# Retention and SoLU feed-forward on one Trainium2 core: the carried state without its zeros, scores and state product in 64x64 quarter arrays, and a new written-out order

## The chip, the cores and the metric

One kernel on one core of a Trainium2 chip. Everything runs in one launch: the inputs lie in the chip's memory, the output goes back there, and the time is device microseconds from the start to the end of one execution. Before the change: median 212.06 us of 3 runs (211.68 to 212.1). The core has a matrix engine (PE, with its weight loads shown as PEld), a vector engine (DVE), an activation engine (ACT), a general engine (POOL) and SP, which here only issues transfers. Each engine works its own list of instructions in order.

## What is computed

Two stages, the second on the output of the first. The attention part is retention: scores weighted by a fixed decay per head, no softmax. There are 8 batches, 8 heads, 576 positions, 64 numbers per head; the feed-forward part has 4608 tokens of 512 and a hidden width of 1024.

```python
scores = q @ k.T / 8                               # per batch and head
Dmat   = where(i >= j, gamma[h] ** (i - j), 0)     # gamma[h] = 1 - 2**(-5-h)
x      = (scores * Dmat) @ v                       # heads side by side: 4608 x 512
h      = x @ w_in                                  # 4608 x 1024
solu   = h * softmax(h)
ln     = (solu - mean) / sqrt(var + 1e-6) * g_ln
out    = ln @ w_out                                # 4608 x 512
```

## The kernel before, in words

**Chunks.** The 4608 tokens are cut into 36 chunks of 128. Two batches form a group of nine chunks: for each of the four stretches of 128 positions one chunk of each batch, and a ninth chunk that holds the last 64 positions of both batches, interleaved. Numbers 8, 17, 26 and 35 are such ninth chunks. Within a batch the retention is done in stretches: inside a chunk by scores, across chunks by a carried state of 64 x 64 per head.

**What one chunk goes through.** Names are those of the steps in the code, and of the tokens in the order. `ld` issues three loads (q, k, v as float32, 256 KB each) on SP. `cq`, `ck`, `cv` make float16 of them, with the decay factors multiplied in for q and v. `tq` transposes q and k on PE in pairs of heads (16 matmuls with an identity); `tr` does only q, for chunks whose k is transposed by a DMA issued in `kd`. `eq` and `er` copy the transposes to `qkT`. `sc` (line 366) computes the scores of 8 heads, `mk` masks them on DVE. `kv` (line 389) multiplies k and v into `kp`, the state's increment; `ad` adds it to the carried state, giving `t`; `dk` (line 417) makes of `t` the float16 state `s16` for the next chunk and `d3` (line 430) the float32 one. `av` (line 441) adds masked scores times v into the accumulator `x`, and `fs` (line 455) adds state times q into the same accumulator. `ex` copies `x` out as `xT`; `m1` multiplies with w_in (for the first chunks in rows, `mr`); `mx`, `xp`, `so`, `sq`, `ra`, `rp` are the maximum, the exponential, the product and the normalisation; `tu` and `eu` transpose the result (`du` does it by DMA for the last chunks); `m2` multiplies with w_out, `st` scales and stores. The last chunk runs the feed-forward in halves (`hm` to `hw`). `wu` are matmuls on a tile of zeros that only keep PE busy at the start, `gt` and `c2` turn the vector g_ln, `li`, `wi`, `lo`, `wo`, `mm`, `mc`, `ws` bring in the weights, convert them and take the mean out of w_out.

**How PE's array is used.** Nearly all products are written as two half products, `HALF` (line 248): the stationary operand has 128 rows and 64 columns, and the two halves give output partitions 0 to 63 and 64 to 127 (`product`, line 255, `turn`, line 250). The profile writes such a group `128*64`. `sc` is the exception: the depth of one head is 64, so it takes 64 rows and 128 columns (`64*128` in the profile), even heads from partitions 0 to 63 into one PSUM bank and odd heads from 64 to 127 into another. `fs` is of the `128*64` kind because its state is kept with zeros: for a pair of heads, `s16` is 128 x 128 with the two 64 x 64 states on the diagonal and zeros beside them. `dk` writes those zeros anew for each chunk, by multiplying with a table `gd` that has them.

**What sets the order.** Nothing is scheduled by the compiler. `ORDER` is a written-out list of tokens `step:chunk[:engine]`, and each engine gets its instructions in the order in which the tokens name them. The letter picks the engine for steps that can run on more than one (a: ACT, v: DVE, g: POOL). SP's list of loads, stores and DMA transposes follows from it as well. `BANKS` gives the PSUM bank for each product in turn, `SLOTS` the buffer for each tile of a ring; `BY_PE` names the chunks from 12 on whose k is transposed by PE instead of by DMA.

Of the kernel before, what the change touches and what calls it, by code (L numbers as in the profile page):

```python
# [29 lines left out]
eq:4:a sc:4 so:1 d3:2 ad:4 ld:3 ck:3:a cq:3:g tq:3 dk:2 ce:1 xp:0 m1:2 mk:4 cv:3:g kv:3 ld:5  # L30
cq:5:g av:4 fs:4 ck:5:g eq:3:a sq:1 so:0 ad:3 ld:6 sc:3 lo:0 cv:5:g ck:6:g ex:4:a tq:5 eq:5:a
cq:6:g mx:2 xp:2 mk:3 dk:3 ce:0 cv:6:g lo:2 m1:4 tu:1 mx:4 sc:5 wu:1:2 eu:1:a mk:5 d3:4 d3:3 av:3
fs:3 xp:4 so:2 tu:0 av:5 wo:1:g ex:3:a kv:5 fs:5 ce:2 tq:6 lo:1 so:4 eu:0:a wo:4:g ce:4 eq:6:a
m1:3 sc:6 ad:5 ex:5:a kv:6 ad:6 wo:3:a wo:2:a lo:3 m1:5 wo:6:v ld:7 tu:2 wo:7:g wo:0:a ld:8 wo:5:a
sq:2 ra:1:g tu:4 mk:6 rp:1 ld:12 mx:3 ld:9 eu:2:v m2:1 sq:0 dk:6 ld:10 dk:4 sq:4 cq:8:g eu:4:v
m2:0 cq:7:v st:1 ck:7:a xp:3 ra:0:v cv:7:v mx:5 so:3 mm:0 ld:11 rp:0 st:0 tq:7 mc:0:v av:6 ld:13
eq:7:a fs:6 ex:6:a m2:2 sc:7 ra:2:g ck:8:g ws:0:v dk:5 ce:3 rp:2 tq:8 xp:5 d3:5 mk:7 so:5 cv:8:g
eq:8:a ra:4:v ws:4:v ws:7:v st:2 m1:6 tu:3 sc:8 mk:8 m2:4 ck:9:g rp:4 sq:3 kv:7 eu:3:a m2:3 cq:9:g
ws:6:v ad:7 dk:7 mx:6 ws:2:g sq:5 ws:5:v ra:3:v rp:3 ws:1:v st:4 ra:5:g cq:11:v av:7 fs:7 ex:7:a
ck:10:g ld:17 tu:5 eu:5:a xp:6 rp:5 ws:3:v cv:9:g av:8 cq:10:g cq:12:g fs:8 ex:8:v so:6 ck:12:g  # L40
tr:9 m1:7 m2:5 ck:11:g er:9:av st:3 tu:6 sc:9 mx:7 m1:8 st:5 eu:6:v xp:7 kd:12 kv:9 ld:14 mk:9
so:7 av:9 sq:6 ex:9:a tr:10 er:10:a cv:10:g ad:9 d3:9 ra:6:v rp:6 cq:13:g sq:7 ra:7:g ck:13:g
kd:13 m2:6 st:6 mx:8 cv:13:g tu:7 eu:7:a sc:10 mk:10 m1:9 kv:10 ad:10 dk:10 tr:11 xp:8 so:8 av:10
ex:10:a tr:12 er:12:v cv:12:g er:11:a m2:7 tu:8 dk:9 sc:11 mx:9 m1:10 cv:11:g mk:11 av:11 fs:11
ld:15 sq:8 rp:7 ra:8:v eu:8:a kv:11 d3:10 xp:9 cq:17:g rp:8 ex:11:a st:7 m2:8 so:9 tu:9 ad:11
d3:11 dk:11 mx:10 sc:12 cq:14:g ck:14:a kd:14 sq:9 m1:11 eu:9:v xp:10 ck:15:g ld:16 st:8 kv:12
mk:12 ld:19 ra:9:v cv:17:g tr:14 er:14:a tr:13 ad:12 dk:12 so:10 av:12 fs:12 ex:12:a cv:14:g
er:13:a m2:9 sc:13 mx:11 rp:9 xp:11 mk:13 cq:16:g tu:10 eu:10:a ck:17:v m1:12 so:11 sc:14 st:9
mk:14 av:13 ck:16:g sq:10 fs:13 ex:13:a m2:10 ra:10:g rp:10 mx:12 d3:12 kv:13 ad:13 cq:15:g tu:11
dk:13 eu:11:v sq:11 kv:14 kd:16 d3:13 ld:18 ra:11:v rp:11 st:10 m1:13 xp:12 ck:19:g tr:15 er:15:a  # L50
ld:21 av:14 ad:14 cv:19:g fs:14 ex:14:a tr:16 er:16:a m2:11 so:12 cv:15:g sc:15 mx:13 mk:15 tu:12
xp:13 m1:14 dk:14 st:11 so:13 eu:12:a cv:16:g kv:15 d3:14 ad:15 sc:16 mk:16 av:15 fs:15 ck:18:g
sq:13 kd:18 mx:14 m2:12 kv:16 ex:15:a tr:17 sq:12 ad:16 ra:12:g rp:12 ra:13:v av:16 fs:16 ld:20
xp:14 ex:16:a tu:13 er:17:v m1:15 so:14 ck:21:g sc:17 eu:13:a mx:15 kd:19 tu:14 st:12 dk:16 mk:17
eu:14:a xp:15 so:15 ld:22 m2:13 cq:18:g tr:18 er:18:a av:17 dk:15 fs:17 ck:20:v ex:17:a m1:16
cq:19:v ld:23 rp:13 st:13 tu:15 sc:18 mx:16 sq:14 ra:14:v eu:15:a m2:14 mk:18 cv:18:g xp:16 so:16
rp:14 cq:21:g cq:20:g st:14 tr:19 er:19:a kd:21 sq:15 ra:15:g rp:15 cq:22:g kv:18 ad:18 m1:17
mx:17 av:18 sq:16 sc:19 mk:19 m2:15 ex:18:a cv:20:g d3:18 ld:24 xp:17 kv:19 ad:19 d3:19 dk:18
tu:16 tr:20 er:20:v tr:21 so:17 cv:21:g eu:16:a er:21:a m1:18 ck:22:g kd:22 av:19 st:15 cq:23:g
# [24 lines left out]
st:26 mx:32 er:35:av ex:34:a sc:35 ad:34 mx:33 xp:32 sq:29 ra:29:g so:32 xp:33 ra:28:g rp:28 du:32
m2:28 rp:29 ra:30:v so:33 du:33 m2:29 dk:34 mk:35 m1:34 mx:34 st:28 sq:31 m2:30 av:35 dk:33 fs:35
sq:32 ex:35:v xp:34 so:34 ra:31:g m2:31 du:34 sq:33 ra:32:v rp:30 hm:35:0 hx:35:0 st:30 hm:35:1
st:29 hx:35:1 m2:32 rp:31 st:31 sq:34 hp:35:0 ho:35:0 ra:33:g hp:35:1 rp:33 ho:35:1 hc:35 m2:33
rp:32 st:32 ht:35:0 he:35:0:v ht:35:1 ra:34:g he:35:1:v hq:35:0:v rp:34 hq:35:1:a ra:35:g st:33
m2:34 st:34 rp:35 h2:35:0 hw:35:0:a h2:35:1 hw:35:1:v
# [13 lines left out]
qf 012345601234560135426015324601532460  # L103
kf 012345012345012453014523014520314520
vf 012345601234560134625016342051346250
q16 012340123401324103123041203412304132
v16 012341023410234132012041320421320413
k16 012345120345102341502314053210452310
qkT 012301230123013120321302310231032103
# [748 lines left out]
```

## Time and profile before

| | |
|---|---|
| median of 3 runs | 212.06 us (211.68 to 212.1) |
| the profiled execution | 212.6 us, of which 210.9 us from the first to the last instruction |
| mean granted clock of PE | 0.997 |
| PE busy | 195.6 us, 93% of the span |
| weight loads (PEld) busy | 124.6 us, 59% |
| DVE busy | 177.8 us, 84% |
| ACT busy | 167.4 us, 79% |
| POOL busy | 166.5 us, 79% |
| moved by DMA | 46.94 MB, mean 223 GB/s |

How to read the rows of the trace: a group of a view by lines shows line, engine, operation, output and inputs, shapes and count, then busy time and the mean of one, then idle time before it and what ended that. A row of the timeline shows the start, the time from the first start to the last end in the row, the engine, the instruction and its count. Matmuls overlap in the pipeline, so the time that a group of matmuls really takes is read from its start to the start of the group behind it, not from its length. In a table by stage, each engine has its busy time and, in brackets, its count of instructions.

### The profile page before, as it was taken

How to read it: one execution, taken by the hardware profiler on the slowest of the kernel's cores; microseconds unless marked ns; L12 is line 12 of the kernel's file. 1: busy time of each engine (PE TensorE's matmuls, PEld its weight loads, DVE VectorE, ACT ScalarE, POOL GpSimd, SP SyncE). 2: the span in 40 equal slices, each digit the busy share in tenths (PEclk: the TensorE clock that was granted, in tenths of full speed). 3: DMA queues.
4: the chain of work that ended last, by engine and by line, in shares of the span. 5: the costliest groups of instructions: out<-in, count | busy, mean ns of one | idle time of the engine just before them, and what ended most of it. 6: DMA issues, size and time to landing. Idle time of an engine off the chain costs nothing.

```text
span 210.9 us, 7674 instructions
## 1 busy us (share of the span) xinstructions
PE 195.6 (93%) x3173; PEld 124.6 (59%) x3173; DVE 177.8 (84%) x312; ACT 167.4 (79%) x289; POOL 166.5 (79%) x244
## 2 busy tenths in 40 slices
PE   0985699999999999999999999999999999999992
PEld 0463467656756666666666656676666666565552
DVE  0474899999998799979898899999989998999650
ACT  2333689989759997988899788888798897798982
POOL 5284898998798998996928999799999975938531
PEclk9999999999999999999999999999999999999998
DMA  5999899999998899999999799999999995999264
GB/s 134 263 324 276 208 243 333 276 219 249 238 236 234 215 218 253 250 222 287 190 227 252 178 221 226 188 251 195 210 271 223 170 210 153 174 168 280 69 215 152
DMA packets 110931, 46.94 MB, mean 223 GB/s; under 512 B 95656, under 2 KB 104880, under 8 KB 110896
## 3 DMA queue, kind: packets, MB, share of 16 engines
q1 hardware_dynamic: 110576, 46.28, 96.7%
q8 instruction: 25, 0.41, 0.9%
q10 hardware_dynamic: 320, 0.16, 0.3%
q14 instruction: 10, 0.08, 0.1%
HBM read 32.54 MB, written 9.44 MB: 199 GB/s over the span
## 4 chain that ended last, share of the span: by engine, by line
PE 75%; SPq 12%; DMA 6%; POOL 2%; issue 1%; ACT 1%; DVE 0%; POOLq 0%; DVEq 0%
PE o L258 28%; PE h L258 24%; SPq L272 6%; PE lp L253 5%; SPq L276 5%; PE sc L373 4%; DMA qf<-in_q_dram 4%; PE x L448 3%; PE x L258 3%; DMA kf<-in_k_dram 2%; PE tr L253 2%; PE tp L253 2%; SPq L771 1%; PE kp L397 1%; PE oh L258 1%
## 5 line engine op out<-in xcount | busy, mean ns | idle before, releaser
L258 PE MATMUL h<-w_in,xT 128*64 128x512 f16 x560 | 66.7, 380 | 1.4 <-DVE w_in L245 1.4
L258 PE MATMUL o<-w_c,uT 128*64 128x512 f16 x480 | 56.8, 380 | 0.0
L386 DVE TENSOR_TENSOR ret<-sc,tris 128x512 f16<-128x512 f32 x72 | 46.1, 681 | 3.3 <-PE sc L373 2.5
L258 PEld LDWEIGHTS <-xT 128*64 128x64 f16 x576 | 31.6, 110 | 24.4 <-issue 1.9
L510 ACT ACTIVATE e<-h,nm 128x1024 f32<-128x1024 f32 x35 | 39.3, 1123 | 7.5 <-DVE nm L504 6.5
L519 DVE SCALAR_TENSOR_TENSOR u<-h,e 128x1024 f16<-128x1024 f32 x35 | 42.6, 1217 | 2.7 <-ACT e L510 2.2
L504 DVE TENSOR_REDUCE nm<-h 128x1 f32<-128x1024 f32 x35 | 42.6, 1217 | 2.1 <-PE h L258 1.8
L258 PEld LDWEIGHTS <-uT 128*64 128x64 f16 x560 | 30.4, 110 | 23.6 <-issue 0.2
L292 POOL TENSOR_TENSOR q<-qf,small 128x512 f16<-128x512 f32 x31 | 32.4, 1051 | 6.8 <-DMA qf<-in_q_dram 6.8
L424 POOL TENSOR_TENSOR s<-t,small 128x512 f16<-128x512 f32 x32 | 33.9, 1063 | 3.5 <-DVE t L412 3.3
L547 ACT ACTIVATE sq<-u,su 128x1024 bf16<-128x1024 f16 x30 | 34.6, 1154 | 1.2 <-DVE u L519 1.1
L281 POOL TENSOR_TENSOR v<-vf,small 128x512 f16<-128x512 f32 x32 | 33.9, 1063 | 1.8 <-DMA vf<-in_v_dram 1.8
L607 ACT ACTIVATE o_sb<-o,rs 128x512 f32<-128x512 f32 x35 | 24.1, 694 | 7.3 <-POOL rs L573 3.8
L573 POOL TENSOR_TENSOR rs<-w,mhalf 128x1 f32<-128x1 f32 x36 | 20.9, 581 | 5.8 <-DVE w L564 3.7
L245 ACT CAST xT<-x 128x512 f16<-128x512 f32 x32 | 18.6, 588 | 5.1 <-PE x L258 4.2
L245 ACT COPY uT<-lp 128x1024 f16<-128x1024 f16 x17 | 17.3, 1019 | 0.7 <-PE lp L253 0.7
L245 POOL CAST k<-kf 128x512 f16<-128x512 f32 x24 | 14.6, 611 | 4.0 <-DMA kf<-in_k_dram 3.9
L253 PE MATMUL lp<-ident,u 128*64 128x128 f16 x448 | 17.1, 220 | 0.1
L436 POOL TENSOR_TENSOR s<-t,small 128x256 f32<-128x256 f32 x24 | 15.0, 630 | 2.1 <-DVE t L412 1.5
L448 PE MATMUL x<-ret,v 128*64 128x128 f16 x288 | 15.2, 225 | 1.3 <-DVE ret L386 1.2
L253 PEld LDWEIGHTS <-q 128*64 128x64 f16 x280 | 10.7, 115 | 9.0 <-POOL q L292 6.5
L245 ACT COPY qkT<-tp 128x512 f16<-128x512 f16 x24 | 13.2, 598 | 3.4 <-PE tp L253 3.3
(88 smaller groups left out, 267.0 us busy)
## 6 DMA issues: line engine op xcount, KB each, us to landing
qf<-in_q_dram SPq DMA_DIRECT2D x36, 256.0 KB, 4.2
kf<-in_k_dram SPq DMA_DIRECT2D x36, 256.0 KB, 4.6
vf<-in_v_dram SPq DMA_DIRECT2D x36, 256.0 KB, 5.0
out_dram<-o_sb SPq DMA_DIRECT2D x35, 256.0 KB, 4.1
w_in<-in_moe_w_in_dram SPq DMA_DIRECT2D x4, 512.0 KB, 7.4
w_out<-in_moe_w_out_dram SPq DMA_DIRECT2D x4, 512.0 KB, 6.2
qkT<-k SPq DMA_TRANSPOSE x19, 4.3
out_dram<-o_sbh ACTq DMA_DIRECT2D x2, 64.0 KB, 2.2
```

The source lines that it names most:

```text
L245: (engine.copy if engine is nc.scalar else engine.tensor_copy)(out=out, in_=in_)
L253: nc.tensor.transpose(out=out[w], in_=in_[:, w], identity=ident)
L258: nc.tensor.matmul(out=out[w], lhsT=lhsT[:, w], rhs=rhs, start=start, stop=stop, skip_group_check=True,)
L281: engine.tensor_tensor(out=dst, in0=T.pop((key, n)), in1=table.unsqueeze(2).to_broadcast([P, H, D]), op=ALU.mult,)
L292: ENG[e].tensor_tensor(out=dst.rearrange("p (a h) d -> p h a d", h=2), in0=T.pop(("qf", n)).rearrange("p (h a) d -> p h a d", h=2), in1=ta ...
L386: nc.vector.tensor_tensor(out=r, in0=s, in1=m, op=ALU.mult)
L424: nc.gpsimd.tensor_tensor(out=s16, in0=t.unsqueeze(2).to_broadcast([P, 4, 2, D]), in1=gd.unsqueeze(3).to_broadcast([P, 4, 2, D]), op=ALU.mult,
L504: nc.vector.tensor_reduce(out=nm, in_=T["h", n], axis=AX.X, op=ALU.max, negate=True)
L510: nc.scalar.activation(out=e, in_=T["h", n], func=ACT.Exp, bias=T.pop(("nm", n)), accum_out=s)
L519: nc.vector.scalar_tensor_tensor(out=u, in0=T.pop(("h", n)), scalar=-1.0, in1=T.pop(("e", n)), op0=ALU.mult, op1=ALU.mult, accum_out=su,)
L547: nc.scalar.activation(out=s, in_=T.pop(("v", n)), func=ACT.Square, scale=-float(DFF), bias=T.pop(("su", n)), accum_out=ss,)
L607: nc.scalar.activation(out=o_sb, in_=T.pop(("o", n)), func=ACT.Copy, scale=T.pop(("rs", n)))
```

## The change

Four things change together.

1. `dk` no longer writes zeros: `s16` becomes 128 x 4 x 64 (the two heads' states one under the other), and the table `gd` goes.
2. `fs` takes the state in quarters: for each pair of heads, rows 0 to 63 give output partitions 0 to 63 and rows 64 to 127 give 64 to 127. The number of matmuls stays 8 (16 in a ninth chunk).
3. `sc` is cut once more along its columns: 16 matmuls of 64 x 64 in place of 8 of 64 x 128.
4. `BY_PE` names four chunks (13, 16, 20, 24) in place of two (15, 20), and `ORDER`, `BANKS` and `SLOTS` are written anew as a whole, with other engines for many steps.

```diff
-BY_PE = (15, 20)
+BY_PE = (13, 16, 20, 24)
...
-        gd[e * 64 : e * 64 + 64, :, e] = gs[e * 64 : e * 64 + 64]
-    small = np.concatenate([gq, gk, gqt, gkt, gs, gd.reshape(P, 8), gqm, par], axis=1).astype(np.float32)
+    small = np.concatenate([gq, gk, gqt, gkt, gs, gqm, par], axis=1).astype(np.float32)
...
     def sc(n):
...
-                nc.tensor.matmul(
-                    out=s[e][:, hp], lhsT=qkT[dd, 1, hp], rhs=qkT[dd, 0, hp],
-                    start=True, stop=True,
-                )
+                for w in HALF:
+                    nc.tensor.matmul(
+                        out=s[e][w, hp], lhsT=qkT[dd, 1, hp, w], rhs=qkT[dd, 0, hp],
+                        start=True, stop=True,
+                    )
...
     def dk(n):
...
-        s16 = ring(stp, [P, 4, 2, D], F16, "s16")
+        s16 = ring(stp, [P, 4, D], F16, "s16")
         nc.gpsimd.tensor_tensor(
-            out=s16, in0=t.unsqueeze(2).to_broadcast([P, 4, 2, D]),
-            in1=gd.unsqueeze(3).to_broadcast([P, 4, 2, D]), op=ALU.mult,
+            out=s16, in0=t, in1=gs.unsqueeze(2).to_broadcast([P, 4, D]), op=ALU.mult
         )
...
     def fs(n):
...
-                product(
-                    part(T["x", n][:, hp], i), s[:, hp].rearrange("p e d -> p (e d)"),
-                    part(qkT[:, 0, hp], i), False, i == len(s16) - 1,
-                )
+                for w in HALF:
+                    nc.tensor.matmul(
+                        out=part(T["x", n][w, hp], i), lhsT=s[w, hp],
+                        rhs=part(qkT[w, 0, hp], i), start=False, stop=i == len(s16) - 1,
+                        skip_group_check=True,
+                    )
```

Two stretches of the order, before and after, from the middle (chunks 12 to 17):

```
before:  ... tr:16 er:16:a m2:11 so:12 cv:15:g sc:15 mx:13 mk:15 tu:12 xp:13 m1:14 dk:14 ... av:15 fs:15 ck:18:g ...
after:   ... av:15 fs:15 rp:12 sc:16 mx:14 ... m2:13 ex:16:v tu:14 ... av:17 fs:17 ex:17:a sq:15 mx:16 sc:18 m2:14 ...
```

Counted over the whole list, PE has 36 `sc` and 28 `fs` in both. In the new list 14 of the `fs` stand directly beside an `sc` among PE's steps, four stand beside another `fs` (two pairs), and ten stand alone. The first nine loads (chunks 1, 0, 2, 4, 3, 5, 6, 7, 8) and the weights among them keep their places on SP, except that the four parts of w_in come in the order 3, 0, 2, 1 (before 2, 3, 0, 1) and the last two of w_out are swapped; behind that the loads come in another order. DMA transposes of keys go from 19 to 17. Of the steps that can move, ACT converts 16 keys (before 9), POOL 15 (before 24), DVE 5 (before 3).

More of the change, by code (lines that the diff above doesn't have):

```diff
@@ L30 @@
[L30 to L59, printed above, removed]
@@ L84 @@
[L84 to L89, printed above, removed]
+c1:0 wu:5:2 ld:1 ld:0 wu:3:2 gt:0 c2:0 cq:1:g ck:1:a tq:1 wu:4:2 eq:1:a ld:2 cv:1:v cq:0:v ck:0:a
@@ new lines @@
+kv:1 sc:1 mk:1 tq:0 eq:0:v li:3 cv:0:g ad:1 cv:2:g kv:0 ad:0 dk:0 d3:0 sc:0 ck:2:a wu:2:2 cq:2:v
+mk:0 li:0 wi:3:0:v tq:2 li:2 eq:2:a av:0 av:1 ex:1:v li:1 kv:2 ad:2 ld:4 d3:1 d3:2 ex:0:a wi:3:1:a
+wi:0:0:a wi:0:1:v sc:2 mk:2 ld:3 mr:1:3 dk:2 mr:0:0 wi:1:0:v ld:5 wi:2:1:a mr:1:0 av:2 dk:1 fs:2
+ex:2:v wi:2:0:a ck:4:a ld:6 mr:1:2 wi:1:1:g mr:1:1 cq:4:g lo:0 mr:0:2 mr:0:1 mr:0:3 tq:4 mx:1 xp:1
+mx:0 eq:4:a cv:4:g so:1 kv:4 cq:3:g ck:3:g sc:4 ad:4 cv:3:g cq:5:g tq:3 ce:1 ck:5:g m1:2 cv:5:g
+kv:3 lo:2 xp:0 mk:4 so:0 ad:3 av:4 fs:4 ce:0 d3:3 lo:3 lo:1 eq:3:a sc:3 mx:2 d3:4 tq:5 sq:1 ck:6:g
@@ new lines @@
+ex:4:a m1:4 eq:5:a dk:3 tu:1 mk:3 av:3 mx:4 sc:5 dk:4 mk:5 xp:2 eu:1:a fs:3 ex:3:a wu:1:2 so:2
+xp:4 so:4 tu:0 kv:5 ad:5 cq:6:g cv:6:g ce:4 av:5 fs:5 ex:5:a ld:7 tq:6 eq:6:a m1:3 ce:2 kv:6 sc:6
+ld:8 wo:6:v eu:0:a ad:6 wo:1:g m1:5 wo:0:a mk:6 wo:4:g ld:10 tu:2 ld:9 tu:4 eu:4:v ra:1:g ld:12
+wo:5:a wo:3:a wo:7:g wo:2:a cq:7:g sq:4 m2:1 mx:3 ck:7:a eu:2:v sq:0 rp:1 tq:7 eq:7:a cv:7:g xp:3
+mx:5 ra:0:v rp:0 dk:5 m2:0 st:0 av:6 cq:8:g sq:2 fs:6 ex:6:v mm:0 so:3 m2:2 ce:3 ld:11 mc:0:v sc:7
+ws:4:v cv:8:v st:1 ck:8:a tq:8 mk:7 xp:5 so:5 ws:0:v m1:6 ra:2:g dk:6 rp:2 ra:4:g eq:8:a sc:8 st:2
@@ new lines @@
+cq:9:g mk:8 tu:3 eu:3:a d3:5 rp:4 m2:4 st:4 ws:7:v kv:7 ad:7 tu:5 eu:5:a ck:9:g ld:13 ws:6:v
+ws:1:v tr:9 er:9:av av:7 fs:7 m2:3 cv:10:g cq:12:g mx:6 dk:7 av:8 fs:8 ws:5:v ws:2:g ex:7:a sc:9
+m1:7 sq:3 ra:3:g ex:8:a xp:6 sq:5 ws:3:v m2:5 mk:9 so:6 tu:6 ld:14 rp:3 cv:9:g st:3 ra:5:v ck:12:v
+mx:7 sq:6 eu:6:v av:9 ex:9:a cq:10:g xp:7 kv:9 ad:9 rp:5 cq:11:g st:5 ra:6:g dk:9 kd:12 ck:10:v
+m1:8 tr:10 er:10:a m2:6 so:7 sq:7 rp:6 mx:8 sc:10 tu:7 eu:7:a st:6 cv:12:v m1:9 xp:8 mk:10 kv:10
+ad:10 ck:11:g cq:14:g tr:11 ra:7:g tr:12 cv:11:g av:10 ex:10:a rp:7 dk:10 ld:15 m2:7 so:8 d3:9
@@ new lines @@
+tu:8 er:11:av mx:9 er:12:a sc:11 m1:10 st:7 kv:11 mk:11 eu:8:a xp:9 ad:11 sq:8 av:11 fs:11 sc:12
+cq:13:g ex:11:a m2:8 so:9 sq:9 mx:10 kv:12 d3:10 cv:14:g cv:13:g ad:12 ld:16 ck:14:g kd:14 m1:11
+ra:8:g tr:14 ck:13:a rp:8 st:8 ck:15:a mk:12 tu:9 av:12 fs:12 tr:13 kd:15 ld:17 xp:10 ra:9:v
+cq:15:v ex:12:a eu:9:v m2:9 er:13:a so:10 er:14:a sc:13 ld:19 rp:9 st:9 tu:10 d3:11 cv:16:g m1:12
+mx:11 mk:13 xp:11 cq:16:g d3:12 av:13 dk:12 so:11 eu:10:a ld:22 sc:14 cv:15:v dk:11 fs:13 sq:10
+ra:10:g ld:18 ck:16:a ex:13:a rp:10 mk:14 sq:11 ra:11:g mx:12 xp:12 m2:10 kv:13 ad:13 dk:13 kv:14
@@ new lines @@
+ad:14 d3:13 tu:11 m1:13 eu:11:v so:12 st:10 av:14 fs:14 ex:14:a tr:16 er:16:a ld:21 tr:15 m2:11
+er:15:v mx:13 xp:13 sc:15 dk:14 ck:17:g cq:19:g ck:19:g rp:11 cq:17:g st:11 cv:17:g tu:12 eu:12:a
+m1:14 ck:22:g mk:15 so:13 kv:15 ad:15 sq:12 ra:12:g d3:14 av:15 fs:15 rp:12 sc:16 mx:14 cq:22:g
+ex:15:a xp:14 cv:18:g ck:18:a kd:18 m2:12 kv:16 cq:18:g ld:20 mk:16 tu:13 dk:15 tr:17 m1:15 kd:19
+ad:16 eu:13:v er:17:a st:12 dk:16 so:14 sq:13 ra:13:g mx:15 xp:15 rp:13 av:16 fs:16 sc:17 m2:13
+ex:16:v tu:14 mk:17 tr:18 so:15 sq:14 ra:14:v er:18:a m1:16 ld:23 eu:14:v rp:14 st:13 av:17 fs:17
@@ new lines @@
+ex:17:a sq:15 mx:16 sc:18 m2:14 mk:18 tr:19 kd:22 xp:16 ck:21:v kd:21 ra:15:v rp:15 ck:20:g
+cq:20:g kv:18 st:14 er:19:v ld:24 tu:15 m1:17 eu:15:a ad:18 av:18 ex:18:a so:16 sq:16 sc:19 mx:17
+mk:19 cv:19:g cv:20:g m2:15 ra:16:v tr:20 xp:17 dk:18 cq:21:g tu:16 cv:22:g av:19 st:15 ex:19:a
+m1:18 kv:19 so:17 eu:16:a er:20:v tu:17 sc:20 ck:23:a ad:19 mx:18 mk:20 eu:17:a xp:18 m2:16 tr:21
+rp:16 kv:20 m1:19 d3:18 av:20 fs:20 er:21:v ad:20 sc:21 sq:17 kd:23 st:16 so:18 sq:18 mx:19 d3:19
+mk:21 m2:17 cv:21:g tu:18 cv:23:v ld:27 cq:23:g ld:25 ex:20:a tr:22 xp:19 kv:21 er:22:a ad:21
@@ new lines @@
+so:19 d3:20 ra:17:g m1:20 mx:20 rp:17 eu:18:a st:17 cv:24:g av:21 dk:19 ra:18:g fs:21 sc:22 mk:22
+rp:18 sq:19 cq:24:v ra:19:g rp:19 ex:21:a ld:26 m2:18 xp:20 so:20 tu:19 dk:20 tr:23 cq:25:g st:18
+ck:27:v ck:25:g kd:25 kv:22 eu:19:a m1:21 av:22 ad:22 er:23:a sc:23 fs:22 ex:22:a mx:21 m2:19
+kv:23 dk:22 ck:24:a ld:28 mk:23 tu:20 tr:24 xp:21 ld:29 d3:21 st:19 ad:23 er:24:a av:23 eu:20:v
+d3:22 dk:21 fs:23 m1:22 ck:26:g cv:25:g so:21 ex:23:a tu:21 eu:21:a kd:27 kv:24 mx:22 xp:22 sc:24
+m1:23 cq:26:g ad:24 cq:27:g tr:27 mk:24 kv:25 er:27:a d3:23 so:22 tr:25 ck:28:g dk:23 kd:28
@@ new lines @@
+er:25:a cv:27:g ld:30 av:24 fs:24 ld:31 cv:26:g ad:25 dk:25 tr:26 tu:22 cv:28:g ex:24:a er:26:a
+mx:23 sc:25 m1:24 mk:25 av:25 fs:25 xp:23 eu:22:a sc:26 dk:24 so:23 ex:25:a mk:26 kv:27 cq:28:g
+tu:23 eu:23:v kv:28 ck:29:g kd:29 ad:28 dk:28 m1:25 ad:27 sq:23 sq:21 d3:27 d3:28 ld:32 av:26
+fs:26 dk:27 cq:29:g sq:22 sq:20 mx:24 xp:24 sc:27 mk:27 m2:21 m2:23 ra:21:v rp:21 st:21 ra:23:v
+tr:28 ra:22:v ck:30:a ex:26:a rp:23 ra:20:g rp:20 rp:22 kd:30 cv:29:v cq:30:g er:28:a cv:30:g
+m2:20 cq:31:g kv:29 so:24 cq:32:g st:23 sc:28 mx:25 m1:26 ad:29 mk:28 sq:24 st:20 tr:29 xp:25
@@ new lines @@
+ck:32:g tr:30 er:30:a av:27 ex:27:a ra:24:v mx:26 kd:32 er:29:a xp:26 m2:22 st:22 so:25 sc:29
+ck:31:v av:28 cv:32:g ex:28:a mk:29 m1:27 kd:31 kv:30 sq:25 so:26 ld:33 tr:32 ld:34 dk:29 tu:25
+eu:25:a tu:24 sq:26 m1:28 ad:30 dk:30 mx:27 d3:29 sc:30 xp:27 rp:24 eu:24:v er:32:a m2:24 st:24
+ra:25:v mk:30 av:29 so:27 tr:31 er:31:a mx:28 av:30 fs:29 ex:29:v fs:30 ex:30:a tu:26 tu:27
+eu:27:v xp:28 cv:31:g kv:31 ad:31 d3:31 ck:33:a m1:30 sc:31 kd:33 so:28 eu:26:a m2:25 rp:25 sq:27
+st:25 mk:31 mx:30 ck:34:a xp:30 cq:33:g d3:30 kv:32 ad:32 sc:32 mk:32 m1:29 mx:29 tr:33 dk:31
@@ new lines @@
+er:33:a av:31 av:32 cq:34:v fs:31 kd:34 kq:34 ld:35 so:30 ex:31:a fs:32 m2:27 cv:33:g du:28 kv:33
+ad:33 ex:32:a sc:33 xp:29 m1:31 m2:26 ra:27:g sq:28 mk:33 rp:27 av:33 so:29 du:29 dk:32 ra:26:g
+mx:31 fs:33 sq:30 st:27 sc:34 ra:28:g sq:29 xp:31 mk:34 so:31 m1:32 ex:33:a du:31 cv:34:g av:34
+fs:34 ck:35:a du:30 ra:29:g cq:35:g tr:35 ex:34:v sq:31 er:35:a kv:34 rp:26 st:26 m1:33 mx:32
+d3:32 ra:30:v m2:28 mx:33 xp:32 ad:34 ra:31:g xp:33 so:32 dk:34 du:32 sq:32 rp:28 st:28 m2:29
+so:33 sc:35 mk:35 sq:33 m1:34 mx:34 m2:31 du:33 rp:30 xp:34 cv:35:g av:35 rp:29 st:29 so:34 du:34
@@ L90 @@
+dk:33 fs:35 ex:35:a ra:33:g rp:33 m2:30 st:30 sq:34 hm:35:0 hx:35:0 rp:31 hm:35:1 st:31 hx:35:1
+hp:35:0 m2:32 ra:32:g m2:33 hp:35:1 ho:35:0 rp:32 st:32 ra:34:g rp:34 ho:35:1 hc:35 hq:35:0:v
+hq:35:1:a ht:35:0 he:35:0:v ht:35:1 he:35:1:v m2:34 ra:35:g rp:35 st:33 st:34 h2:35:0 h2:35:1
+hw:35:0:a hw:35:1:v
 """
 BANKS = """
-01231023102130121321302130213023110231012320132012302301320310312031201320321021312310210231032032
-10230123012031203123123031231023102301201023012021032103213013021301023102130213013202130213012103
@@ L95 @@
-130132132132130210321032132123230212103201032301231031
+01230132132010321032103210321013201302023102301310320321023012032031301231230103213021330120123012
+31021023120123012302301230312031023102313201320321302203120312031201320132013021321032132032012312
+032012301201230130230123012301201232132103023123013213
 """
@@ L102 @@
 SLOTS = """
[L103 to L109, printed above, removed]
-ret0 012301230123012301230123012301230120
-ret1 012301230123012301230123012301230120
-t 01230120231023102301230123102310
-xT 012301230123012301230123012301230123
-s16 01230213210312031230123012031203
-h 010101010101010101010101010101010101
-s32 012302103210321032102310
+qf 012345601234560134250613245016325041
+kf 012345012345012453021453021453210453
+vf 012345601234560123450621304256314025
+h 010101010101010101010101010101010101
+q16 012340123401234120342132013420413204
+k16 012345012345021350412350245310543210
+qkT 012301230123013020132301032130321031
+v16 012341023410231420132401320413240132
+ret0 012310231023102310231023102310231023
+ret1 012310231023102310231023102310231023
+t 01231201302130123012301320312031
+s16 01230123012301320132013021031203
+s32 012302130213021302130213
+xT 012301230123012301230123012301230213
 e 01201201201201201201201201201201201
-u 01234021340213402134021343210432103
-uT 01234012340123401234012341302143021
+u 01234031240312403124031242310243104
+uT 01234013240132401324013241203142031
 o_sb 01230123012301230123012301230123012
@@ L138, in _np_tables @@
     gs = np.zeros((P, 4))
-    gd = np.zeros((P, 4, 2))
     for e in range(2):
@@ L206, in fours @@
         )
-    small = const.tile([P, 54], FP, name="small")
+    small = const.tile([P, 46], FP, name="small")
     tris = const.tile([P, 2, P], FP, name="tris")
@@ L224 @@
     gs = small[:, 32:36]
-    gd = small[:, 36:44].rearrange("p (a b) -> p a b", a=4)
-    gqm, par = small[:, 44:52], small[:, 52:54]
+    gqm, par = small[:, 36:44], small[:, 44:46]
     banks = iter("".join(BANKS.split()))
```

29 lines of the change are left out of this document (removed).

## Prediction

> **What bounds the kernel now.** I read the page first (busy shares), then the table by stage, then PE's timeline in one stretch. The shares alone decide nothing: PE leads, but DVE, ACT and POOL are all near 80%.
>
> ```profile
> PE 195.6 (93%) x3173; PEld 124.6 (59%) x3173; DVE 177.8 (84%) x312; ACT 167.4 (79%) x289; POOL 166.5 (79%) x244
> ```
>
> The table by stage (us, then busy time and count of PE, PEld, DVE, ACT, POOL, then clock, DMA share, GB/s) says more.
>
> ```profile
> 5.40:23.10 17.70, 13.87 (x177) 8.95 (x179) 10.02 (x19) 5.84 (x10) 9.93 (x13) 1.00 1.02 268
> 23.10:47.30 24.20, 22.16 (x391) 14.41 (x387) 23.75 (x42) 22.27 (x40) 22.38 (x29) 1.00 1.12 268
> 47.30:100.00 52.70, 52.55 (x898) 33.63 (x899) 48.28 (x89) 45.54 (x79) 46.55 (x64) 1.00 1.02 240
> 100.00:150.00 50.00, 49.90 (x880) 32.48 (x876) 46.51 (x80) 43.68 (x73) 43.71 (x58) 1.00 1.04 212
> 150.00:207.30 57.30, 57.17 (x842) 35.16 (x838) 48.53 (x83) 48.73 (x89) 40.99 (x72) 1.00 0.90 195
> 207.30:210.90 3.60, 0.00 (x0) 0.00 (x0) 0.47 (x1) 0.00 (x0) 0.00 (x0) 0.80 0.43 149
> ```
>
> From 47.3 to 207.3 us PE is idle for 0.15 + 0.10 + 0.13 = 0.4 us out of 160. Up to 23.1 us loads set the pace (DMA share 1.02 with PE idle 3.8 of 17.7); from 23.1 to 47.3 PE is idle 2.0 us, and all engines are close to full. So from about 23 us on, what is added to PE's list is added to the end, and what is taken from another engine gives nothing unless PE waits for it. The last 3.6 us are the output's way out.
>
> The timeline of PE shows what its groups cost. I take the time from one group's start to the next one's.
>
> ```profile
> 99.99 0.61 PE L253 MATMUL lp<-ident,u 128*64 128x128 f16 x16
> 100.44 1.89 PE L258 MATMUL h<-w_in,xT 128*64 128x512 f16 x16
> 102.27 0.40 PE L373 MATMUL sc<-qkT 64*128 64x128 f16 x8
> 102.59 0.64 PE L253 MATMUL lp<-ident,u 128*64 128x128 f16 x16
> 103.06 1.89 PE L258 MATMUL o<-w_c,uT 128*64 128x512 f16 x16
> 104.79 0.39 PE L253 MATMUL tr<-ident,q 128*64 128x128 f16 x8
> 105.01 0.39 PE L448 MATMUL x<-ret,v 128*64 128x128 f16 x8
> 105.24 0.61 PE L258 MATMUL x<-qkT,s 128*64 128x64 f16 x16
> 105.66 1.92 PE L258 MATMUL h<-w_in,xT 128*64 128x512 f16 x16
> 107.41 0.61 PE L253 MATMUL lp<-ident,u 128*64 128x128 f16 x16
> 107.96 0.40 PE L373 MATMUL sc<-qkT 64*128 64x128 f16 x8
> 108.28 1.92 PE L258 MATMUL o<-w_c,uT 128*64 128x512 f16 x16
> 110.03 0.39 PE L253 MATMUL tr<-ident,q 128*64 128x128 f16 x8
> 110.26 0.29 PE L397 MATMUL kp<-v,k 128*64 128x64 f16 x8
> 110.38 1.90 PE L258 MATMUL h<-w_in,xT 128*64 128x512 f16 x16
> ```
>
> Undisturbed, 16 matmuls of 512 columns take 1.73 (103.06 to 104.79), 16 of 128 columns 0.45 (99.99 to 100.44), 8 of 128 columns 0.22 (104.79 to 105.01), 8 of 64 columns 0.12 (110.26 to 110.38), and a ninth chunk's 16 of 64 columns with a step 0.42 (105.24 to 105.66). Two halves run at once: a pass of two matmuls of 128 columns takes 0.45 / 8 = 0.056 us.
>
> Round each `sc`, the only group of another shape (64*128), this breaks. The group before takes 0.10 longer (1.83 at 100.44, 0.55 at 107.41). `sc` itself takes 0.32, though its 8 matmuls are four passes of 128 columns like those of `tr` (0.22): 0.10 more. The group behind takes 0.02 longer (0.47 at 102.59, 1.75 at 108.28). PE empties before the shape changes and again before it changes back: one **visit** to the other shape costs 0.22 to 0.23 us beyond its matmuls; I use 0.225. `sc` never stands beside another `sc`, so there are 36 visits:
>
> ```profile
> 5.40:47.30 41.90, 3.21 (x56) 1.82 (x56) 1.00 1.08 268
> 47.30:207.30 160.00, 11.51 (x232) 6.61 (x232) 1.00 0.98 215
> ```
>
> These two rows are the same table for the line of `sc` alone: 56 / 8 = 7 visits up to 47.3 us and 232 / 8 = 29 behind it. `fs` (x<-qkT,s) needs none: it has the common shape.
>
> **The change, part by part.**
>
> *The state without zeros.*
>
> ```profile
> L424 POOL TENSOR_TENSOR s<-t,small 128x512 f16<-128x512 f32 x32 | 33.9, 1063 | 3.5 <-DVE t L412 3.3
> L436 POOL TENSOR_TENSOR s<-t,small 128x256 f32<-128x256 f32 x24 | 15.0, 630 | 2.1 <-DVE t L412 1.5 <-DVE t L410 0.6
> L258 PE MATMUL x<-qkT,s 128*64 128x128 f16 x192 | 9.3, 219 | 0.0
> ```
>
> `dk` (L424) halves in size; its like is `d3` (L436) at 630 ns, so POOL saves 32 x (1063 - 630) = 13.9 us. On the path that is worth nothing: `fs`, which waits for that state, stands in the last row with 0.0 us of idle time before it. POOL's 166.5 us lie beneath PE's full list, and a shorter `dk` leaves only POOL idle.
>
> *`fs` in quarters.* The same 8 matmuls, two at once (they use different rows and different columns), so 0.22 as before, but their shape is now 64x64: unless it stands beside `sc`, each `fs` is a visit.
>
> *`sc` in quarters.* 16 matmuls of 128 columns. If the four quarters run at once this is again four passes, 0.22. Its issue is bounded by the rows: `kp` gets 8 loads and matmuls through in 0.12, so 16 need at most 0.24 to 0.25, 0.02 to 0.03 over; times 36 that is 0 to 1.0 us. I take 0, since a pass of `kp` is itself nearly as long as its 64 columns need by the 0.056 of 128.
>
> *The price of a visit to 64x64.* No row of before shows this shape. Below it is bounded by 0 (halves following halves show no wait at all), above I know no dearer change than that of `sc`. I take 0.225, the nearest row: as with `sc`, half the rows are used in place of all, and in and out of it PE has to change the rows.
>
> *Counting visits.* I went through both lists and counted runs of `sc` and `fs` with nothing of PE between. Before: 36. After: 22 `sc` alone, 14 pairs of `sc` and `fs`, 2 pairs of `fs`, 10 `fs` alone, 48 in all. Up to 23.1 us, where PE waits for loads anyway, there are three before (chunks 1, 0, 2) and four after (the `fs` of chunk 2). That leaves 33 and 44 in the stretch where PE is full: 11 more, 11 x 0.225 = **2.5 us**.
>
> *Keys by PE.* Two more chunks transpose k on PE: 2 x 0.22 = **0.45 us**. In exchange two DMA transposes go, and ACT or DVE copies two more halves.
>
> ```profile
> qkT<-k SPq DMA_TRANSPOSE x19, 4.3
> L245 ACT COPY qkT<-tr 128x512 f16<-128x512 f16 x15 | 8.8, 589 | 0.3 <-PE tr L253 0.3
> ```
>
> The transposes of 4.3 us each were issued early enough that PE did not wait for them; their going frees SP's list and some DMA, which is worth nothing while PE is full. Two copies of 0.59 us come to ACT's load.
>
> *The new order.* Seven more conversions of keys go to ACT, with the copies some 7 us: 167 becomes 175 of a span of over 210. DVE changes by about 1 us, POOL loses about 21. All stay beneath PE's list, which is 47 + 160 us long; if that cover fails anywhere, the stall is PE's and counts in full. Loads: the first nine and the weights keep their place on SP, and w_in is still four pieces in a row. The wait that ends the start is for w_in,
>
> ```profile
> PE h L258 <- DVE w_in L245: 1.4, 1, 1.4
> POOL q L292 <- DMA qf<-in_q_dram: 6.8, 5, 2.7
> ```
>
> and then for the loads behind it (`cq` on POOL, up to 2.7 us at once). Neither moves. `wu` and `gt` now stand ahead of the first transposes, in time that PE spends waiting for the first q; `dk` and `d3` of the first chunks come off POOL sooner, which the loads hide. The start: 0, within 1 us either way.
>
> *Sum.* 2.5 + 0.45 = 2.95 us, on the profiled execution's 212.6: 215.5. The profiled execution is 0.5 above the median of 212.06, so the forecast is **215.0 us**, 1.4% more.
>
> The Trainium skill, "TensorEngine Tiling (Array Packing)", section Key Properties, says that changing the tiling mode, and not just the tile, drains the engine. By that rule 64x64 is a mode of its own, and each visit pays; the sum would be the one above, and by it a free visit (first rival) is unlikely. The trace agrees for 64*128, with the 0.225 us shown, and is silent on 64x64.
>
> **The rivals.**
>
> *The visit is free or cheap (faster).* If PE can take quarters behind halves without emptying, because each quarter lies wholly within a half's columns, all 33 visits of before vanish: -33 x 0.225 = -7.4, + 0.45 = -7.0, **205.1 us**. At half the price (the wait on one side alone) it is 44 x 0.112 - 7.4 + 0.45 = -2.0, **210.0 us**. The point from which it decides: 44p + 0.45 = 7.4, a price p of 0.158 us. For it: no row shows this change of shape. Against it: `sc` also lies in rows that the halves contain, and pays. 0.10 for free, 0.10 for about half.
>
> *Quarters take turns (slower still).* The two quarters of `fs` come from different rows and go to the same PSUM bank (`x`); the two row halves of `sc` of before went to two banks, so no row shows rows sharing one. If they take turns, 24 `fs` take 0.45 in place of 0.22 and 4 of the ninth chunks 0.84 in place of 0.42: 5.5 + 1.7 = 7.2 more, **222 us**. The same page of the Trainium skill, section Gotcha 1: PSUM Pressure, says that different row tiles cannot access one PSUM bank at the same time; nothing in this trace can show whether they would wait, and by that rule the sum would be these 222. Against it: the two quarters write different partitions, as halves do, and halves share a bank at full speed. 0.10.
>
> *The order starves PE.* From 23.1 to 47.3 us DVE is busy 23.75, ACT 22.27 and POOL 22.38 of 24.20, and ACT gets more to do. A step that is late there, or one of the loads now in another order behind chunk 8, stops PE. The order before loses 2.0 us there and 0.4 later; twice that, 2 to 4 us more, gives **217 to 219.5 us**. 0.12.
>
> **How the numbers follow.** Forecast with its own range 213.5 to 217 (issue of `sc`, 1 us at the start either way): 0.58. Free 0.10, half price 0.10 (209.5 to 213), turns 0.10, starving 0.12. A range of 209.5 to 219.5 holds the forecast, the half price and the starving, 0.80, and leaves out the free visit and the turns. About 0.2% (0.4 us) is what a measurement of this kernel can tell from no change. Faster by more: 0.10 and 0.08 of the half price, 0.18; within: 0.02; slower: 0.58 + 0.10 + 0.12 = 0.80.
>
> **What would show it.** In the profile after, PE's timeline has `sc` with 16 matmuls of 64x64. Right: the group ahead of each visit is 0.10 longer, the last group of the visit takes about 0.32, an `fs` alone 0.32 too, an `fs` ahead of an `sc` 0.22; PE idle stays near 0.4 us after 47 us; POOL's row for `s` falls to about 20 us at 630 ns. Wrong: no step in PE's group times round `sc` and `fs` (first rival); `fs` at 0.45 (turns); idle PE in the table by stage with DVE, ACT or a load as the releaser (starving).

## The result, and the profile after

The changed kernel takes 215.78 us (median of 4 runs, 214.31 to 218.01) against 212.08 us of before beside it: ratio 1.0131, 95% interval 1.009 to 1.0172. The run of 218.01 us, at a clock of 0.968 against 0.998 to 1.0 in the other three, is a slow one and is not in the ratio, which is therefore smaller than that of the two medians. A second set of runs (experiment 9) gave 1.0117 (1.0079 to 1.0154). The forecast was 215.0 us, 1.4% slower. The profiled execution took 215.55 us (before: 212.6), 213.8 of it from first to last instruction (before: 210.9).

The page's first part of the changed kernel, and the rows behind 47.3 us of its table by stage (the last of them moved with the end), with the columns as in the prediction:

```profile
PE 200.5 (94%) x3477; PEld 127.0 (59%) x3477; DVE 180.7 (85%) x311; ACT 173.8 (81%) x301; POOL 146.7 (69%) x235
```

```profile
47.30:100.00 52.70, 52.70 (x950) 33.04 (x948) 48.77 (x83) 47.15 (x81) 41.46 (x66) 1.00 1.03 232
100.00:150.00 50.00, 49.79 (x983) 33.27 (x980) 46.80 (x80) 43.75 (x75) 38.63 (x56) 1.00 0.98 221
150.00:210.10 60.10, 60.03 (x936) 36.35 (x931) 49.44 (x88) 52.80 (x96) 35.81 (x65) 1.00 0.80 182
```

POOL lost 20 us, most of it in the state's step, as foretold (33.9 us at 1063 ns before):

```profile
L422 POOL TENSOR_TENSOR s<-t,small 128x256 f16<-128x256 f32 x32 | 20.6, 648 | 6.0 <-PE o L255 2.4
```

ACT gained 6, and PE is as full as it was: 0.3 us idle behind 47.3 us (0.4 before). It simply has more to get through. Where, its timeline shows. First a state product that stands alone and a group of scores that stands alone (start us, length, instruction, count; a group's cost is again from its start to the next one's):

```profile
80.91 0.39 PE L445 MATMUL x<-ret,v 128*64 128x128 f16 x8
81.23 0.41 PE L466 MATMUL x<-qkT,s 64*64 64x128 f16 x8
81.57 0.41 PE L250 MATMUL tp<-ident,q 128*64 128x128 f16 x8
81.81 0.39 PE L250 MATMUL tp<-ident,k 128*64 128x128 f16 x8
82.11 1.92 PE L255 MATMUL o<-w_c,uT 128*64 128x512 f16 x16
83.95 0.42 PE L371 MATMUL sc<-qkT 64*64 64x128 f16 x16
84.30 0.64 PE L250 MATMUL lp<-ident,u 128*64 128x128 f16 x16
84.77 1.46 PE L255 MATMUL h<-w_in,xT 128*64 128x512 f16 x12
```

`av` (x<-ret,v) ahead of the lone `fs` takes 0.32 in place of 0.22, `fs` itself 0.34, `tp` behind it 0.24. That is 0.10 + 0.12 + 0.02 beyond the matmuls: one visit, 0.24 us. In halves, `fs` cost 0.22 and its neighbours nothing extra. From the profile before:

```profile
91.21 0.39 PE L448 MATMUL x<-ret,v 128*64 128x128 f16 x8
91.43 0.39 PE L258 MATMUL x<-qkT,s 128*64 128x128 f16 x8
91.65 0.39 PE L253 MATMUL tr<-ident,q 128*64 128x128 f16 x8
```

The scores take 0.35 here, 0.02 to 0.03 more than in their old shape; with 1.84 for `o` ahead of them (1.73 undisturbed) and 0.47 for `lp` behind (0.45) their visit costs 0.11 + 0.13 + 0.02 = 0.26. And a pair, `fs` with `sc` behind it:

```profile
75.75 0.39 PE L445 MATMUL x<-ret,v 128*64 128x128 f16 x8
76.07 0.30 PE L466 MATMUL x<-qkT,s 64*64 64x128 f16 x4
76.16 0.24 PE L371 MATMUL sc<-qkT 64*64 64x128 f16 x2
76.20 0.22 PE L466 MATMUL x<-qkT,s 64*64 64x128 f16 x2
76.23 0.22 PE L371 MATMUL sc<-qkT 64*64 64x128 f16 x2
76.26 0.22 PE L466 MATMUL x<-qkT,s 64*64 64x128 f16 x2
76.29 0.41 PE L371 MATMUL sc<-qkT 64*64 64x128 f16 x12
76.63 1.92 PE L255 MATMUL o<-w_c,uT 128*64 128x512 f16 x16
```

From 76.07 to 76.63 the two take 0.56 for matmuls worth 0.45: they share one visit.

A measure that needs no start and no end: from the third product with w_out (`m2` of chunk 2, ahead of which both lists have done the same work) to the last product (`h2`). The two rows for before and then for after:

```profile
47.34 1.92 PE L258 MATMUL o<-w_out,uT 128*64 128x512 f16 x16
...
205.25 1.91 PE L258 MATMUL oh<-w_c,uTh 128*64 128x256 f16 x32
```

```profile
47.70 1.25 PE L255 MATMUL o<-w_out,uT 128*64 128x512 f16 x10
...
208.11 1.91 PE L255 MATMUL oh<-w_c,uTh 128*64 128x256 f16 x32
```

205.25 - 47.34 = 157.91 us before, 208.11 - 47.70 = 160.41 after: 2.50 us of the 2.9 by which the spans differ. I call this the **full stretch**. It holds 29 visits before and 38 after. The rest of the 2.9 is mostly a later start, 47.70 against 47.34.

### The profile page after: what moved, and what is told of

Its sections match the earlier page's. It is cut to its first block, busy times and chain, and to the rows that moved or that the text cites. A ratio compares the mean times of both kernels' runs of the same rounds, so it can differ in the third digit from the quotient of the medians.

```text
span 213.8 us, 8287 instructions
## 1 busy us (share of the span) xinstructions
PE 200.5 (94%) x3477; PEld 127.0 (59%) x3477; DVE 180.7 (85%) x311; ACT 173.8 (81%) x301; POOL 146.7 (69%) x235
## 4 chain that ended last, share of the span: by engine, by line
PE 79%; DMA 8%; SPq 6%; ACT 3%; issue 1%; DVE 1%; POOL 0%; DVEq 0%
PE o L255 29%; PE h L255 24%; PE lp L250 5%; DMA w_out<-in_moe_w_out_dram 5%; PE sc L371 4%; PE x L466 4%; DMA w_in<-in_moe_w_in_dram 4%; PE x L445 3%; PE tp L250 3%; SPq L273 2%; SPq L269 2%; PE tr L250 2%; PE kp L395 1%; SPq L770 1%; ACT e L509 1%; SPq L780 1%
## 5 line engine op out<-in xcount | busy, mean ns | idle before, releaser
L255 PEld LDWEIGHTS <-xT 128*64 128x64 f16 x576 | 30.9, 110 | 24.7 <-issue 2.1
L255 PEld LDWEIGHTS <-uT 128*64 128x64 f16 x560 | 29.9, 110 | 25.8 <-issue 1.1
L278 POOL TENSOR_TENSOR v<-vf,small 128x512 f16<-128x512 f32 x30 | 31.4, 1050 | 10.0 <-DMA vf<-in_v_dram 9.7
L422 POOL TENSOR_TENSOR s<-t,small 128x256 f16<-128x256 f32 x32 | 20.6, 648 | 6.0 <-PE o L255 2.4
L242 ACT CAST xT<-x 128x512 f16<-128x512 f32 x30 | 17.6, 589 | 5.8 <-PE x L466 3.2
L242 ACT COPY qkT<-tp 128x512 f16<-128x512 f16 x32 | 17.2, 587 | 3.4 <-PE tp L250 3.3
L371 PE MATMUL sc<-qkT 64*64 64x128 f16 x576 | 17.3, 227 | 1.3 <-ACT qkT L242 1.0
L563 POOL TENSOR_SCALAR w<-ss,w 128x1 f32<-128x1 f32 x20 | 5.8, 292 | 15.7 <-ACT sq L546 14.5
L250 PEld LDWEIGHTS <-u 128*64 128x64 f16 x448 | 14.3, 110 | 2.6 <-issue 0.4
```

The source lines that it names most:

```text
L242: (engine.copy if engine is nc.scalar else engine.tensor_copy)(out=out, in_=in_)
L250: nc.tensor.transpose(out=out[w], in_=in_[:, w], identity=ident)
L255: nc.tensor.matmul(out=out[w], lhsT=lhsT[:, w], rhs=rhs, start=start, stop=stop, skip_group_check=True,)
L278: engine.tensor_tensor(out=dst, in0=T.pop((key, n)), in1=table.unsqueeze(2).to_broadcast([P, H, D]), op=ALU.mult,)
L371: nc.tensor.matmul(out=s[e][w, hp], lhsT=qkT[dd, 1, hp, w], rhs=qkT[dd, 0, hp], start=True, stop=True,)
```

## The experiments

My theory: PE's list sets the end from 47 us on, and each change from the common shape to a row-split one and back costs about 0.24 us, whatever it is spent on. Rivals: the new order costs the time and the shapes are free; POOL's relief is worth something that the change lost elsewhere; the extra time round the scores is not the change of shape. All ratios are against runs of before on the same chip, with 95% intervals.

**1. The new shapes in the old order.** Before, with the three edits of shape and nothing else (`sc`, `dk`, `fs` of the diff above).

> The old order with the new shapes: the state without zeros, its product and the scores in quarters, nothing else. In that order the quarters make 58 visits of PE to the other shape (31 scores alone, 21 state products alone, 5 pairs, 1 double), of which 54 lie behind 23 us, in place of 33. Theory (each visit costs PE about 0.24 us, and PE's list sets the end): 54 x 0.24 - 33 x 0.228 = 5.4 us more than before, about 217.5 us. Rival (the new order and its other engines cost the time, the shapes are free): the time of before, 212.1 us, or less, since POOL has 13.9 us less to do.

Ratio **1.0228** (1.0178 to 1.0277). The full stretch:

```profile
48.01 1.05 PE L258 MATMUL o<-w_out,uT 128*64 128x512 f16 x8
...
210.27 1.91 PE L258 MATMUL oh<-w_c,uTh 128*64 128x256 f16 x32
```

162.26 us, 4.35 more than before. Of the 58 visits 47 lie in it: 47 x 0.24 - 29 x 0.228 = 4.7. The order is that of before, the time goes with the visits, and 13.9 us less on POOL did not show. That the shapes are free is refuted.

**2. Before with the light state alone.** `dk` writes half as much; `fs` stays in halves and reads the same 64 columns twice:

```diff
-        s16 = ring(stp, [P, 4, 2, D], F16, "s16")
+        s16 = ring(stp, [P, 4, D], F16, "s16")
...
-            out=s16, in0=t.unsqueeze(2).to_broadcast([P, 4, 2, D]),
-            in1=gd.unsqueeze(3).to_broadcast([P, 4, 2, D]), op=ALU.mult,
+            out=s16, in0=t, in1=gs.unsqueeze(2).to_broadcast([P, 4, D]), op=ALU.mult
...
+                for w in HALF:
+                    nc.tensor.matmul(
+                        out=part(T["x", n][w, hp], i), lhsT=s[:, hp],
+                        rhs=part(qkT[:, 0, hp], i), start=False, stop=i == len(s16) - 1,
...
```

> Before, with the state kept without zeros and half the work in that step on POOL, but the state product still in halves: the zeros are left out of the product, so it adds the other head's part as well; every shape on PE is that of before. Theory (PE's list sets the end, POOL's time is worth nothing): POOL falls to about 153 us and the time stays at 212.1 us, within 0.5. Rival (POOL's relief is worth time, and the change lost more elsewhere): clearly faster, by 1 us or more.

```profile
L424 POOL TENSOR_TENSOR s<-t,small 128x256 f16<-128x256 f32 x32 | 20.0, 630 | 2.2 <-DVE t L412 2.0
```

POOL's step fell from 33.9 to 20.0 us and the ratio is **1.0019** (0.9985 to 1.0053): nothing gained. In the old order POOL's time is worth nothing.

**3. The new order with the old shapes.** The changed kernel with `sc`, `dk` and `fs` put back as in before.

> The new order, banks, slots and keys, but with the old shapes: the state with its zeros (POOL works 13.9 us more), its product in halves, the scores in 64x128. Theory (visits): 36 visits again, 33 of them where PE is full, so 44 x 0.24 - 33 x 0.228 = 3.0 us less than the changed kernel, about 212.5 us, with 0.45 us of keys still in it. Rival (the order): it keeps the changed kernel's 215.5 us or goes above it, since POOL is fuller.

Ratio 1.010 (1.0047 to 1.0154): slower than expected (0.2%), and little faster than the changed kernel. Visits alone do not explain this. Run once more on another chip:

> The new order with all old shapes once more, on the same chip as the changed kernel with the zeros; its profile was of the slowest of six executions (217.0 us, the others 214.2 to 215.6). Theory: ratio 1.010 again, the stretch of PE from the third product with w_out to the last product about 159.5 us, with a wait for POOL in it. Rival (chance): ratio 1.003, as with the light POOL.

Ratio **1.0139** (1.0109 to 1.0169). So the new order with 29 visits is as slow as with 38, when POOL writes the zeros. The longest wait of PE behind 47 us, in the first of the two profiles and then in the second (each has one more, of 0.4 us, for DVE):

```profile
PE kp L397 <- POOL v L281: 1.6, 1, 1.6
```

```profile
PE o L258 <- ACT o_sb L607: 1.3, 1, 1.3
```

The changed kernel has a single wait there, of 0.2 us. The wait named in the expectation as POOL's came in the first profile; in the second it is ACT's store, which itself had waited for POOL (`rs`).

**4. The new order, old shapes on PE, light POOL.** As 3, with the state of experiment 2.

> The new order with every shape on PE that of before (scores in 64x128, state product in halves), but the state kept without zeros, so that POOL is as light as in the changed kernel; the zeros are left out of the product, which adds the other head's part as well. The new order with all old shapes had come out 1.0% above before, where the visits and keys alone give 0.2 to 0.3%. Theory (that 1.0% is POOL's 13.9 us of zeros, which the new order has no room for): 36 visits and a light POOL give only the keys, 0.45 us above before, ratio 1.002, and PE shows no wait for POOL behind 47 us. Rival (the new order is worse by itself): ratio stays at 1.010.

Ratio **1.0028** (0.9997 to 1.006), with its full stretch at

```profile
46.80 1.89 PE L255 MATMUL o<-w_out,uT 128*64 128x512 f16 x16
...
204.95 1.91 PE L255 MATMUL oh<-w_c,uTh 128*64 128x256 f16 x32
```

158.15 us, 0.24 above before with the two extra keys in it (0.45 by the sum). The second profile of experiment 3, with the same list on PE and the zeros on POOL, takes 160.90 us there (46.85 to 207.75): 2.75 more, 1.7 of it in its two waits. With 29 visits and POOL light, the new order is as fast as the old one, within what can be measured. It isn't worse by itself: it needs a light POOL.

**5. The changed kernel with the zeros still written.** Shapes and order as changed; `dk` as before, `fs` reads `s[w, hp, e]`, the two quarters on the diagonal.

> The changed kernel, order and shapes as they are, but the state is written with its zeros again: POOL does 13.9 us more, the state product reads the two quarters that lie on the diagonal. The new order with all old shapes had lost 0.7% against the same order with a light POOL. Theory (the new order has no room for the zeros on POOL): about 1.5 us above the changed kernel, ratio 1.018 to 1.020, with waits of PE for POOL behind 47 us. Rival (that loss was peculiar to the old shapes, or chance): the changed kernel's ratio, 1.012 to 1.013.

Ratio **1.0209** (1.0178 to 1.024), against 1.0117 and 1.0131 for the changed kernel: 0.8 to 0.9%, some 1.8 us, for 13.6 us more on POOL (160.3 against 146.7). In the profiled execution the full stretch takes 163.24 us (46.81 to 210.05), 2.8 more than the changed kernel's. PE's waits behind 47 us that the changed kernel does not have make 2.2 of it:

```profile
PE o L258 <- ACT o_sb L610: 1.5, 1, 1.5
PE x L470 <- POOL s L425: 0.7, 1, 0.7
```

and how the first comes about, in POOL's and then in ACT's timeline:

```profile
153.40 1.05 POOL L425 TENSOR_TENSOR s<-t,small 128x512 f16<-128x512 f32 x1
154.41 1.05 POOL L292 TENSOR_TENSOR q<-qf,small 128x512 f16<-128x512 f32 x1
155.40 1.52 POOL L576 TENSOR_TENSOR rs<-w,mhalf 128x1 f32<-128x1 f32 x2
```

```profile
156.44 0.69 ACT L610 ACTIVATE o_sb<-o,rs 128x512 f32<-128x512 f32 x1 [2.27 <-POOL rs L576]
```

POOL works without a gap; its small `rs` stands behind a state with zeros and a conversion, ACT's store waits 2.27 us for it, and PE waits for the bank that this store empties.

**6 and 7. Visits doubled, without any change of order.** Before, with one pair of 64-column matmuls of the common shape in each group of scores: in its middle (visits doubled), and ahead of it (the control, with `hp == 0` in the second line).

```diff
         for hp in range(4):
+            if hp == 2:
+                for w in HALF:
+                    nc.tensor.matmul(
+                        out=s[0][w, 3, 0:64], lhsT=ident[:, w], rhs=ident[:, 0:64],
+                        start=True, stop=True,
+                    )
             for e in range(2):
```

> Before, with one pair of 64-column matmuls of the common shape put in the middle of each group of scores (it writes a part of the scores' bank that the group itself overwrites later): PE leaves the scores' shape and comes back, so 72 visits in place of 36, 66 in place of 33 where PE is full. Theory: 33 x (0.228 + 0.03 for the pair itself) = 8.5 us more, ratio 1.040. Rival (what is lost around the scores is not the change of shape, but their own loads or the start of a group): only the pair's own 1.0 us, ratio 1.005.

> The control for the split scores: the same pair of matmuls, put ahead of each group of scores, where the common shape still holds: 36 visits as before. Both theories: the pair's own 0.03 us and its issue, 33 x 0.03 = 1.0 us, ratio 1.005.

Ratios **1.0302** (1.0263 to 1.0341) and **1.0021** (0.9994 to 1.0048): the same matmuls, and only their place differs. The timelines, split and then control:

```profile
102.89 1.89 PE L258 MATMUL h<-w_in,xT 128*64 128x512 f16 x16
104.72 0.29 PE L379 MATMUL sc<-qkT 64*128 64x128 f16 x4
104.93 0.22 PE L373 MATMUL sc<-ident 128*64 128x64 f16 x2
105.08 0.28 PE L379 MATMUL sc<-qkT 64*128 64x128 f16 x4
105.30 0.64 PE L253 MATMUL lp<-ident,u 128*64 128x128 f16 x16
105.77 0.60 PE L258 MATMUL o<-w_c,uT 128*64 128x512 f16 x4
```

```profile
100.36 1.89 PE L258 MATMUL h<-w_in,xT 128*64 128x512 f16 x16
102.09 0.20 PE L373 MATMUL sc<-ident 128*64 128x64 f16 x2
102.22 0.40 PE L379 MATMUL sc<-qkT 64*128 64x128 f16 x8
102.55 0.64 PE L253 MATMUL lp<-ident,u 128*64 128x128 f16 x16
103.02 0.81 PE L258 MATMUL o<-w_c,uT 128*64 128x512 f16 x6
```

From `h` to `o` 2.88 against 2.66: the second visit costs 0.22 us, with no load of scores and no start of a group in it. The third rival falls. The full stretch takes 164.40 us (47.84 to 212.24) against 158.02 (47.58 to 205.60): 6.38 us, or 29 visits at 0.22. I had expected 33. The four of chunks 4, 3, 5 and 6, between 23 and 47 us, would make 0.9 us, but the stretch starts only 0.26 later; starts vary by more than that among the profiles here (46.80 to 48.34), so how much of the 0.9 arrives is not settled.

**8. Wide scores beside quarter products.** The changed kernel with `sc` back in 64x128.

> The changed kernel with the scores back in 64x128, the state product left in quarters: the 14 pairs then go from one row-split shape to another. If PE empties whenever rows or columns of the shape change, each pair pays about half a visit more, 14 x 0.11 = 1.6, less 0.02 on each of the scores' groups (0.7): about 216.4 us. If only the split of the rows counts, there is no extra change within a pair: about 214.8 us.

Ratio 1.0134 (1.0084 to 1.0183), not told apart from the changed kernel. But its timeline shows what the ratio can't:

```profile
74.91 0.39 PE L444 MATMUL x<-ret,v 128*64 128x128 f16 x8
75.24 0.41 PE L465 MATMUL x<-qkT,s 64*64 64x128 f16 x8
75.58 0.40 PE L370 MATMUL sc<-qkT 64*128 64x128 f16 x8
75.91 1.92 PE L255 MATMUL o<-w_c,uT 128*64 128x512 f16 x16
```

The pair takes 0.34 + 0.33 = 0.67 in place of 0.56. The change from 64x64 to 64x128 costs time too. This 0.11 on the 12 pairs of the full stretch, less 0.02 on each of its 17 lone scores, makes 1.0 us; the stretch takes 161.10 us (46.99 to 208.09), 0.7 more than in the profile of the changed kernel and 0.9 more than in that of experiment 9.

**9. The changed kernel again**, as a measure for the others.

> The changed kernel once more, on the same chip as the others and with more rounds, as their measure: ratio 1.013 to 1.014.

Ratio 1.0117 (1.0079 to 1.0154). Its full stretch takes 160.24 us (47.37 to 207.61), against 160.41 in the first profile.

## Why the prediction was right, point by point

- *What bounds the kernel.* Right: PE is full from 47 us on in every run in which POOL does not write the zeros in the new order (idle at most 0.8 us, in experiment 2). "From about 23 us on" was too early: of 0.9 us that the doubled visits between 23 and 47 us add in experiment 6, only 0.26 is seen at 47 us, and that lies within the spread of the profiles.
- *Counting visits.* 48 against 36 is right. I put 11 more where PE is full; in the full stretch it is 9 (29 to 38).
- *The price of a visit.* Taken as 0.225 from `sc`; measured 0.24 for a lone `fs`, 0.26 for lone scores in quarters, 0.22 for the second visit of experiment 6. That 64x64 pays like 64x128 was a choice without a row; the traces after bear it out, and the rivals of a free or half-priced visit are refuted by `av` at 0.32 and `fs` at 0.34. The Trainium skill's rule that a change of tiling mode drains the engine ("TensorEngine Tiling (Array Packing)", section Key Properties) agrees with what is seen here (0.24), and for 64x64 against 64x128 as well (0.67 in place of 0.56).
- *`sc` in quarters.* Bounded by 0 and 1.0 us, taken as 0: it is 0.02 per group, 29 x 0.02 = 0.6 us in the full stretch, contained in the 0.26 above. This term was mis-sized, and that it makes up for the two visits too many (0.45) is luck.
- *`fs` in quarters.* Right: 0.34 with its drain, not the 0.45 and more of quarters that take turns, though both row halves write one bank. The Trainium skill's rule that different row tiles cannot access one PSUM bank at the same time ("TensorEngine Tiling (Array Packing)", section Gotcha 1: PSUM Pressure) is not borne out here: the quarters write different partitions, and at 0.34 they do not take turns.
- *Keys.* 0.45 by count; the new order with two more keys, 29 visits and a light POOL (experiment 4) is 0.24 above before in the full stretch. The difference of 0.2 is not traced; both lists leave PE idle for a few tenths.
- *POOL's relief worth nothing.* Right in the old order (experiment 2), wrong as a statement on the new one: there the lack of it costs 0.8 to 0.9% (experiment 5). The forecast did not suffer, since it compared before with after and not the edits one by one, but the two parts were not independent: the new order spends what the light state frees.
- *The sum.* 2.95 us by the prediction. By the prices measured, 38 visits at 0.24 against 29 at 0.228 make 2.5, with the keys 2.95; the full stretch shows 2.50, and 2.33 in the profile of experiment 9. Experiment 4 divides it: 0.24 for the order with its keys, and 2.1 to 2.3 for the visits. What is missing, 0.45 to 0.6 us, I have not traced. That the two profiled executions differ by just 2.95 (215.55 - 212.6) is luck: 0.36 of it is the later start of the full stretch, and in experiment 9 it starts at 47.37, as before.
- *The order starves PE.* It does not in the changed kernel, but it does as soon as POOL has the zeros to write: the condition of that rival was POOL, not ACT, where I looked.
- *What can be told from no change.* Put at 0.2%; the intervals of these runs reach 0.3 to 0.5% to each side, so ratios like 1.0019 and 1.0028 are not told from 1.

A version faster than before was not found. It would have to make fewer visits than 36, for instance with the scores of two chunks side by side. That wasn't tried; whether enough PSUM banks are free for it at those points is not shown here.

## What to carry to other kernels

When one engine is full, count what each edit adds to that engine's list, and count changes of array shape as instructions: here each trip to another shape cost as much as 8 matmuls of 128 columns. Work taken from an engine that is not last is worth only what the order can make of it, so try the saving alone in the old order, and the new order without the saving. If groups of a rare shape must exist, put them side by side in one and the same shape: a pair in 64x64 took 0.56 us, the same pair in two shapes 0.67.
